# Last block in an order of its own with stores on two queues; a third of block 2's convolution taps by accumulating DMA

## The chip, the core and the metric

The kernel runs on one core of a Trainium2 chip. The core has a matrix engine (TensorE, PE in the profile), VectorE (DVE), ScalarE (ACT), GpSimd (POOL) and SyncE (SP), each with a queue of its own that it works off in order, and 16 DMA engines that all queues share. Waits between engines are semaphores. The metric is device time in microseconds. The median of three runs of the kernel before is 2315.04 us (2314.68 to 2315.27).

## The reference

A causal convolution over seven taps, with one softmaxed filter for each of eight groups of 24 channels, followed by a feed-forward layer with SiLU:

```python
# x: (8, 4096, 192), weight: (8, 7); moe_w_in: (192, 2048), moe_w_out: (2048, 192)
w = np.exp(weight - weight.max(-1, keepdims=True)); w = w / (w.sum(-1, keepdims=True) + 1e-9)
x_pad = np.concatenate([np.zeros((8, 6, 192)), x], axis=1)
idx = np.arange(4096)[:, None] + np.arange(7)[None, :]
out = np.einsum('hk,bskhg->bshg', w, x_pad[:, idx, :].reshape(8, 4096, 7, 8, 24))
h = out.reshape(32768, 192) @ moe_w_in
y = (h / (1 + np.exp(-h))) @ moe_w_out
```

## The kernel before

**Tiling.** The 32768 tokens are worked in 32 blocks of 1024, numbered `b` = 0 to 31, each as two halves of 512 tokens. The 192 channels are three thirds of 64 rows, `k` = 0, 1, 2. A block is loaded (`ld.k`, L156) into a buffer `nat`, of which there are two, so blocks `b` and `b + 2` share one. VectorE turns it (`i.k`, L490) into `xt`, of which there is one; `ha.0` copies the six halo columns (L512). Seven taps (`v.ki`, L526 to L534) make the convolution of third `k`, back in `nat`; `sp.k` (L556) spreads it into `dup`, and `w.i` (L573, L576) makes sums of it in `win`.

**The two matrix products** are done by fast-multiplication schemes that trade products for sums. The weights are combined once, at the start: `combine` by GpSimd (L138) for the groups of the first product, `combine_out` (25 sums) for the second. Block 0 is done plainly, since its weights are not combined yet: `up_plain` (L609) and `down_plain` (L884, the steps `dp`), its output copied by ScalarE (`cp.k`, L899), turned by VectorE (`op.k`, L907) and stored by SyncE (`stp.k`, L916). From block 1 on, `P`, `L` and halves of them are products (L668, L685), `u` ScalarE copies out of PSUM into a pool of ten `u` buffers (L717), `X`, `a`, `b` sums on VectorE (L711), `S` SiLUs (L729); then `t`, `tC`, `tD` (and `tA` on GpSimd) are sums of the SiLU's output (L793), `Q` the 80 products of the second matrix (L804), `O`, `C`, `d` ScalarE copies (L839, L841), `m.i` VectorE sums (L852), `o.i` transposes (L860) and `st.i` four stores each (L867). Each `Q` writes one of the two halves of PSUM's partitions, and two that write different halves can run side by side.

**Taps.** Each tap is a product of a shifted `xt` by a factor for each row. In blocks 1 and 2 ScalarE makes the first tap in a PSUM bank (L526) and VectorE adds the other six (L534). From block 3 on ScalarE makes every product (L529) into a `u` buffer and GpSimd issues a DMA that adds it onto `nat` (L530); the first of the seven goes to `nat` directly. The buffer comes free when the DMA lands, and a DMA onto the same `nat` waits for the one before.

**The order** is written out by hand as strings of steps. Everything that is issued is kept in program order on its engine. `START` does the rest of block 0 along with blocks 1 and 2; in it a bare step belongs to block 2, `-` to block 1, `=` to block 0, `+` to block 3. Then `PLAN` is gone through once for each block, with the prefixes `-`, `=`, `~`, `+`, `*` for one, two, three blocks back and one, two ahead, and for three blocks past the end, so that block 31's last steps run with nothing beside them, in the order that `PLAN` has for every block. The last two groups of weight sums (`both_sides(GROUPS - 1)`, `both_sides(NJ - 1)`: 22 and 19 sums) are issued ahead of `START`.

**In `START`** block 2's taps on VectorE are the last thing before block 0's transposes `op`. SyncE stores block 0 (twelve DMAs) before it issues the other two thirds of block 3's load, and block 3's transposes stand on VectorE ahead of the sums that PE waits for.

Of the kernel before, what the change touches and what calls it, by code (L numbers as in the profile page):

```python
# [17 lines left out]
def kernel(  # L18
# [24 lines left out]
    nc = tc.nc  # L43
# [8 lines left out]
    NK = D // R  # L52
# [4 lines left out]
    NB = NT // TT  # L57
    NCH = DFF // P
    NM = NCH // 2
    NJ = NM // 2  # L60
# [48 lines left out]
        "=dp.10 =dp.11 -v.26 -v.01 -v.02 -v.03 =dp.12 -v.04 =dp.13 -v.05 -v.06 =dp.14 =dp.15 "  # L109
        "=dp.16 -sp.2 =dp.17 =dp.18 =dp.19 =dp.20 -sp.0 i.2 i.1 =dp.21 =dp.22 =dp.23 =dp.24 "  # L110
        "i.0 =dp.25 =dp.26 =dp.27 =dp.28 =dp.29 =dp.30 ha.0 =dp.31 =dp.32 =dp.33 =dp.34 +ld.1 "
        "-w.0 -w.1 =dp.35 =dp.36 v.00 =dp.37 =dp.38 -w.2 -w.3 -w.4 -w.5 =dp.39 =dp.40 =dp.41 "
        "v.01 =dp.42 v.20 =dp.43 =dp.44 v.02 v.03 v.10 v.11 v.12 v.13 v.14 v.15 v.16 v.04 v.05 "
        "v.06 v.22 v.23 v.24 v.25 v.26 =dp.45 =cp.0 =dp.46 =dp.47 =cp.1 v.21 =cp.2 =op.0 =op.1 "
        "=op.2 =stp.0 =stp.1 =stp.2"
    )
    QUEUE = (0, 4, 1, 2, 3)
    CHAIN_BANKS = (
# [11 lines left out]
    def pin(ins):  # L130
        return tc.keep_in_program_order(ins)
# [13 lines left out]
    nats, xts, gs = {}, {}, {}  # L145
# [35 lines left out]
    warm = const.tile([P, 1], F32, name="warm")  # L181
# [9 lines left out]
    pool = Pinned(nc.gpsimd)  # L191
# [142 lines left out]
    def comb(out, u, v, op):  # L334
        pool.tensor_tensor(out, u, v, op=op)
# [3 lines left out]
    def raw(g, i, k, e):  # L339
        a, j, own = chunks(g)[i]  # L340
        return rows(wr[j] if own == e else ws[j], e)[:, a, k, :]

    def combine(g, e):

        def op(sign, to, u, v):
            comb(raw(g, *to, e), raw(g, *u, e), raw(g, *v, e), ALU.add if sign > 0 else ALU.subtract)

        if (g, e) == (SWAP[0], 0):
            op(-1, (2, 1), (1, 0), (1, 2))
            op(-1, (2, 1), (2, 1), (0, 0))  # L350
            op(-1, (2, 1), (2, 1), (0, 1))
        for order in COMBINE[e]:
            op(*order)

    COMBINE = (
        (
# [158 lines left out]
    CONV_BANKS = (2, 3, 4)  # L515
    taken = {}

    def conv(b, k, i):

        src = xts[b][:, k, i : i + TB]  # L520
        dst = nats[b][:, k, :, :].rearrange("p k c -> p (k c)")
        tap = taps[:, k, i : i + 1]
        taken[b, k] = taken.get((b, k), 0) + 1
        acc = banks[CONV_BANKS[k]] if b in (1, 2) else dst
        if i == 0:
            pin(nc.scalar.activation(acc, src, AF.Copy, scale=tap))  # L526
        elif b > 2:
            z = free.pop(0)
            pin(nc.scalar.activation(z, src, AF.Copy, scale=tap))  # L529
            pin(nc.gpsimd.dma_start(out=dst, in_=z, accum_op=ALU.add))  # L530
            free.append(z)
        else:
            pin(
                nc.vector.scalar_tensor_tensor(  # L534
                    out=dst if taken[b, k] == K else acc,
                    in0=src,
                    scalar=tap,
                    in1=acc,
                    op0=ALU.mult,
                    op1=ALU.add,  # L540
                )
            )
# [49 lines left out]
    def rows(t, e):  # L592
        return t[R * e : R * e + R]
# [29 lines left out]
    cmbs, banks = {}, []  # L623

    GROUPS = 5
    SWAP = (4, 14)

    def chunks(g):
        if g == GROUPS - 1:
            return [(1, i, 1) for i in range(3)]  # L630
        return [(0, g, 0), (1, g, 0), (0, g, 1)]
# [99 lines left out]
    def silu_plain(b, i):  # L731
        cols = slice((i - 1) * TB // 2, i * TB // 2) if i else slice(0, TB)
        h = h_of(b, None, int(i > 0))[:, cols]
        pin(nc.scalar.activation(h, plain_bank(b, i)[:, cols], AF.Silu))
# [121 lines left out]
    def turned(i):  # L856
        return mid(2 + i).rearrange("p (k c) -> p k c", c=SQ)

    def turn_out(b, i):
        pin(nc.vector.transpose(mid(2 + i), mid(i - 1)))  # L860

    def store_out(b, i):
        for q in range(P // SQ):
            third, n = OUT_OF[i][q // 2]
            c = R * third + SQ * (q % 2)
            pin(
                nc.sync.dma_start(  # L867
                    out=out_v[2 * b + n][:, :, c : c + SQ],
                    in_=turned(i)[SQ * q : SQ * q + SQ, :, :],
                )  # L870
            )
# [50 lines left out]
    did = set()  # L922
    BACK = {"-": 1, "=": 2, "+": -1, "~": 3, "*": -2}

    def step(b, token):

        if token[0] in BACK:
            b, token = b - BACK[token[0]], token[1:]
        name, _, arg = token.partition(".")
        if b < 0 or b >= NB or (b, token) in did:  # L930
            return
        did.add((b, token))
        digits = [int(c) for c in arg] if arg.isdigit() else []
        if name[0] == "P":
            product(b, digits[0], int(name[1:]))
        elif name == "L":
            plain(b, *digits)
        elif name == "SL":
            silu_plain(b, *digits)
        elif name[0] in "uXabS":  # L940
            sums_h(b, name, *digits)
        elif name[0] == "Q":
            out_product(b, int(name[1:]), *digits)
        elif name[:2] == "tA":
            sum_g(b, int(name[2:]), slice(0, NJ - 1), nc.gpsimd)
        elif name[:2] == "tB":
            sum_g(b, int(name[2:]), slice(NJ - 1, NJ), nc.vector)
        elif name[:2] in ("tC", "tD"):
            i = NJ // 2 if name[1] == "D" else 0
            sum_g(b, int(name[2:]), slice(i, i + NJ // 2), nc.vector)  # L950
        elif name[0] == "t":
            sum_g(b, int(name[1:]), slice(0, NJ), nc.vector)
        elif name in ("O", "C", "d"):
            out_copy(b, token)
        elif name == "m":
            out_sum(b, *digits)
        elif name == "o":
            turn_out(b, *digits)
        elif name == "st":
            store_out(b, *digits)  # L960
        elif name == "dp":
            next(downs)
        elif name == "cp":
            copy_plain(b, *digits)
        elif name == "op":
            turn_plain(b, *digits)
        elif name == "stp":
            store_plain(b, *digits)
        elif name == "go":
            pool.tensor_copy(warm, nats[1][:, digits[0], 0, 0:1])  # L970
            for g in (2, 3):
                for e in range(2):
                    combine(g, e)
        elif name == "ld":
            load(b, digits)
        else:
            {"i": turn_in, "ha": halo_in, "v": conv, "sp": spread, "w": win}[name](
                b, *digits
            )
# [54 lines left out]

    def both_sides(g):
        for e in range(2):
            combine(g, e)

    def some(ups, n):
        for _ in range(n):  # L1040
# [11 lines left out]
    for j, at in ((1, (2,)), (2, (1, 3)), (3, (2,))):  # L1052
# [9 lines left out]
            swapped(3)  # L1062
        if j < NJ - 1:
            both_sides(j)
    both_sides(GROUPS - 1)
    both_sides(NJ - 1)
    for t in [*(f"i.{k}" for k in range(NK)), "ha.0"]:
        step(1, t)
    rounding(7)
# [4 lines left out]
    did.update((0, t.lstrip("-=+~*")) for t in plan)  # L1074
    for t in START.split():
        step(2, t)
    for b in range(1, NB + 4):
        for t in plan:
            step(b, t)


# [28 lines left out]
```

## Time and profile before

| | us |
|---|---|
| median of 3 runs | 2315.04 (2314.68 to 2315.27) |
| the profiled execution | 2315.82 |
| its span, first to last instruction | 2314.1 |
| PE busy | 2288.6 |
| VectorE busy | 2009.3 |
| ScalarE busy | 1550.2 |
| GpSimd busy | 652.4 |

All times below are counted from the start of the span. Matmuls overlap, two in different halves at once, so a busy PE is one on which at least one product runs. `PEld` is PE's loading of weights. `SPq` is SyncE's DMA queue. In a row of the timeline stand start, length, engine, line, operation, what it writes and reads, how many; in brackets how long the engine had been idle and what released it. In a group row stand the count, then the busy time and the mean of one in ns, then the idle time before.

### The profile page before, as it was taken

The page shows a single profiled execution, that of the slowest core. Times are in us where ns is not written, and L with a number is a line of the kernel's source. Part 1 is how long each engine was busy: PE and PEld are TensorE (multiplying, and loading weights), DVE is VectorE, ACT ScalarE, POOL GpSimd, SP SyncE. Part 2 cuts the span into 40 slices and gives each one's busy share as a digit, 9 for nine tenths or more (in the row PEclk, how much of TensorE's full clock was granted, in tenths as well). Part 3 has the DMA queues.
Part 4 walks back from the last instruction along what each step waited for, and adds up shares of the span by engine and source line. Part 5 has one row for each costly group of instructions (what it writes and reads, how often), then busy time and mean ns, then how long its engine had stood idle before and what let it go on. Part 6 is the DMA issues. An engine that isn't in the chain of part 4 may idle for free.

```text
span 2314.1 us, 31693 instructions
## 1 busy us (share of the span) xinstructions
PE 2288.6 (99%) x10622; PEld 922.3 (40%) x10622; DVE 2009.3 (87%) x2271; ACT 1550.2 (67%) x2836; POOL 652.4 (28%) x728
## 2 busy tenths in 40 slices
PE   9999999999999999999999999999999999999997
PEld 4344433444333444334444334443334443344432
DVE  8878888988889888889888889888898888898887
ACT  6267666776666776667776667766677766677642
POOL 5922223222223222233222232222232222332100
PEclk9999999999999999999999999999999999999999
DMA  7355577665667655677655776656676556765411
GB/s 167 69 94 91 97 122 128 113 106 97 107 117 130 107 103 96 115 124 121 107 96 98 123 128 109 104 100 109 117 129 104 102 96 117 126 119 94 75 17 19
DMA packets 526275, 242.65 MB, mean 105 GB/s; under 512 B 431840, under 2 KB 436960, under 8 KB 526112
## 3 DMA queue, kind: packets, MB, share of 16 engines
q0 software_dynamic: 75616, 138.45, 35.3%
q1 hardware_dynamic: 449440, 102.04, 24.8%
q8 instruction: 84, 1.38, 0.2%
q14 instruction: 79, 0.65, 0.1%
q10 hardware_dynamic: 1056, 0.13, 0.0%
HBM read 31.46 MB, written 25.17 MB: 24 GB/s over the span
## 4 chain that ended last, share of the span: by engine, by line
PE 95%; DVE 3%; SPq 1%; ACT 0%; issue 0%; DMA 0%; DVEq 0%
PE ps L804 46%; PE ps L668 44%; PE ps L685 3%; DVE ps L534 1%; DVE two L138 1%; PE ps L994 1%; PE ps L609 0%; SPq L916 0%; DVE mh L138 0%; SPq L156 0%; PE ps L448 0%; DVE t L793 0%; DMA nat<-in_x_dram 0%; ACT g L138 0%; DVE nat L534 0%
## 5 line engine op out<-in xcount | busy, mean ns | idle before, releaser
L530 POOL DMA_DIRECT2D nat<-u x522 | 447.6, 933 | 1244.2 <-ACT u L529 858.6
L804 PE MATMUL ps<-g,wall 128*64 128x512 f32 x1984 | 743.1, 595 | 0.0
L668 PE MATMUL ps<-win,wr 64*128 64x512 f32 x1550 | 685.8, 598 | 2.4 <-ACT u L717 2.4
L668 PE MATMUL ps<-win,ws 64*128 64x512 f32 x1550 | 644.2, 593 | 0.4 <-ACT u L717 0.4
L717 ACT COPY u<-ps 128x512 f32<-128x512 f32 x775 | 439.6, 590 | 109.4 <-issue 58.9
L804 PE MATMUL ps<-g,wx 128*64 128x512 f32 x1240 | 414.5, 592 | 0.0
L668 PE MATMUL ps<-dup,wr 64*128 64x512 f32 x868 | 402.6, 591 | 0.0
L804 PE MATMUL ps<-t,wall 128*64 128x512 f32 x992 | 368.0, 594 | 0.5 <-DVE t L793 0.5
L529 ACT ACTIVATE u<-xt,taps 128x512 f32<-128x512 f32 x522 | 353.9, 716 | 0.7
L668 PEld LDWEIGHTS ps<-win,wr 64*128 64x128 f32 x1550 | 256.0, 186 | 221.0 <-issue 131.5
L711 DVE TENSOR_TENSOR g<-u,ps 128x512 f32<-128x512 f32 x465 | 309.7, 683 | 31.5 <-PE ps L668 29.2
L729 ACT ACTIVATE g<-ps 128x512 f32<-128x512 f32 x465 | 279.9, 602 | 39.6 <-PE ps L668 39.0
L668 PEld LDWEIGHTS ps<-win,ws 64*128 64x128 f32 x1550 | 257.1, 187 | 121.5 <-issue 94.5
L729 ACT ACTIVATE g<-g 128x512 f32<-128x512 f32 x465 | 280.9, 631 | 34.5 <-DVE g L711 34.5
L804 PEld LDWEIGHTS ps<-g,wall 128*64 128x64 f32 x1984 | 215.7, 137 | 220.9 <-issue 211.7
L711 DVE TENSOR_TENSOR ps<-u,ps 128x512 f32<-128x512 f32 x310 | 214.9, 694 | 92.4 <-PE ps L668 33.1
L668 PE MATMUL ps<-dup,ws 64*128 64x512 f32 x682 | 271.2, 591 | 7.4 <-DVE ps L711 7.4
L804 PE MATMUL ps<-t,wx 128*64 128x512 f32 x744 | 267.0, 594 | 1.3 <-ACT ps L841 1.3
L793 DVE TENSOR_TENSOR t<-g 128x512 f32<-128x512 f32 (+1 forms) x186 | 240.9, 1309 | 5.0 <-DVE g L793 0.5
L839 ACT COPY cmb<-ps 64x512 f32<-64x512 f32 x124 | 72.1, 581 | 238.7 <-PE ps L804 215.6
L793 DVE TENSOR_TENSOR t<-g,t 128x2048 f32<-128x2048 f32 x93 | 212.9, 2290 | 9.0 <-PE ps L804 7.8
L804 PEld LDWEIGHTS ps<-g,wx 128*64 128x64 f32 x1240 | 129.5, 137 | 210.1 <-issue 210.1
(103 smaller groups left out, 2477.3 us busy)
## 6 DMA issues: line engine op xcount, KB each, us to landing
nat<-u POOLq DMA_DIRECT2D x522, 256.0 KB, 4.2
dup<-nat SPq DMA_DIRECT2D x345, 128.0 KB, 2.6
nat<-in_x_dram SPq DMA_DIRECT2D x382, 64.0 KB, 3.9
out_dram<-yx SPq DMA_DIRECT2D x248, 64.0 KB, 2.1
out_dram<-cmb SPq DMA_DIRECT2D x124, 64.0 KB, 4.5
raw<-in_moe_w_out_dram SPq DMA_DIRECT2D x8, 384.0 KB, 4.6
g<-in_moe_w_in_dram SPq DMA_DIRECT2D x8, 192.0 KB, 5.3
ws<-wr POOLq DMA_DIRECT2D x8, 192.0 KB, 4.9
```

Source lines behind the costliest of these rows:

```text
L138: return lambda *args, **kw: pin(getattr(self.engine, name)(*args, **kw))
L529: pin(nc.scalar.activation(z, src, AF.Copy, scale=tap))
L530: pin(nc.gpsimd.dma_start(out=dst, in_=z, accum_op=ALU.add))
L534: nc.vector.scalar_tensor_tensor(out=dst if taken[b, k] == K else acc, in0=src, scalar=tap, in1=acc, op0=ALU.mult, op1=ALU.add,)
L668: nc.tensor.matmul(to[:, cols], raw(g, *LEFT[e][r], e), rhs[:, cols], start=first, stop=True, skip_group_check=True,)
L685: nc.tensor.matmul(plain_bank(b, n and 1 + e)[:, cols], rows(wr[j] if own == e else ws[j], e)[:, a, k, :], rows(dups[b], e)[:, SLOT[e][2 * ...
L711: pin(nc.vector.tensor_tensor(out_, u, v, op=op))
L717: pin(nc.scalar.copy(us[b, g, o][:, cols], t1[:, cols]))
L729: pin(nc.scalar.activation(h, src, AF.Silu))
L793: pin(engine.tensor_tensor(g_part(to, js), g_part(u, js), g_part(v, js), op=op))
L804: nc.tensor.matmul(out_bank(node), out_form(OUT_FORMS[r])[:, j, :], g_part(OPERAND[r], j), start=first, stop=True, skip_group_check=True,)
L839: pin(nc.scalar.copy(to(), out_bank(node)))
```

## The change

Three things.

1. Third `k` = 2 of block 2 is convolved as in the blocks from 3 on: ScalarE makes the first tap in `nat` and six products in `u` buffers, and GpSimd issues six accumulating DMAs. VectorE's six taps for it go. Thirds 0 and 1 of block 2 stay on VectorE.
2. The 41 weight sums that were issued ahead of `START` become a generator `late`, and steps `go.n` in `START` take them from it, the first digit of `n` being the count: 13 ahead of `v.21`, then 5, 5, 5, 5, 4 and 4, with one of the taps `v.22` to `v.26` between each two. On GpSimd the sums keep their order, and the six DMAs stand among them: behind the 13th, 18th, 23rd, 28th, 33rd and 37th. The taps `v.20` to `v.26` now come before `w.0`, and so before `v.00` and `v.10` on ScalarE.
3. The steps of block 31 that `FINISH` names (its 80 `Q`, nearly all its `t`, the copies, `m`, `o`, `st`, and the last few SiLUs and sums ahead of them) are held back while `PLAN` runs, and done after it in `FINISH`'s order. Of the four stores of each `st.i` in block 31, the second and fourth are issued by ScalarE's queue. The steps of block 30 that stood among them come earlier, its last transpose `o.3` and stores `st.3` among them.

In the built programs the order of PE, VectorE and ScalarE between block 3 and block 31's `Q` products is the same as before.

```diff
-        "-w.0 -w.1 =dp.35 =dp.36 v.00 =dp.37 =dp.38 -w.2 -w.3 -w.4 -w.5 =dp.39 =dp.40 =dp.41 "
-        "v.01 =dp.42 v.20 =dp.43 =dp.44 v.02 v.03 v.10 v.11 v.12 v.13 v.14 v.15 v.16 v.04 v.05 "
-        "v.06 v.22 v.23 v.24 v.25 v.26 =dp.45 =cp.0 =dp.46 =dp.47 =cp.1 v.21 =cp.2 =op.0 =op.1 "
-        "=op.2 =stp.0 =stp.1 =stp.2"
+        "go.9 go.4 v.20 v.21 go.51 v.22 go.52 v.23 go.53 v.24 go.54 v.25 go.41 v.26 go.42 -w.0 "
+        "-w.1 =dp.35 =dp.36 v.00 v.10 =dp.37 =dp.38 -w.2 -w.3 -w.4 -w.5 =dp.39 =dp.40 =dp.41 "
+        "v.01 =dp.42 =dp.43 =dp.44 v.02 v.03 v.11 v.12 v.13 v.14 v.15 v.16 v.04 v.05 v.06 "
+        "=dp.45 =cp.0 =dp.46 =dp.47 =cp.1 =cp.2 =op.0 =op.1 =op.2 =stp.0 =stp.1 =stp.2"
+    )
+    FINISH = (
+        "Q17.1 Q4.0 S1.2 Q17.0 Q4.3 S0.0 Q17.3 Q3.0 Q17.2 a0.2 S5.2 S4.2 Q4.1 Q4.2 O.0 tC3 "
+        "Q6.0 Q12.0 Q3.1 Q12.1 Q11.2 Q3.2 Q11.3 tC4 S0.2 tD2 C.0 tD4 tD3 Q5.1 Q12.3 Q5.0 t5 "
...
+        "m.0 d.A Q8.1 d.B Q2.0 d.b Q7.1 m.4 m.1 Q8.0 o.2 Q1.2 Q7.2 m.2 Q2.1 Q19.2 Q2.3 m.5 "
+        "st.2 Q8.3 Q8.2 o.1 st.1 m.3 o.3 st.3"
     )
...
         def op(sign, to, u, v):
             comb(raw(g, *to, e), raw(g, *u, e), raw(g, *v, e), ALU.add if sign > 0 else ALU.subtract)
+            return g
...
         for order in COMBINE[e]:
-            op(*order)
+            yield op(*order)
...
-        acc = banks[CONV_BANKS[k]] if b in (1, 2) else dst
+        by_dma = b > 2 or (b, k) == (2, NK - 1)
+        acc = dst if by_dma or not b else banks[CONV_BANKS[k]]
         if i == 0:
             pin(nc.scalar.activation(acc, src, AF.Copy, scale=tap))
-        elif b > 2:
+        elif by_dma:
             z = free.pop(0)
             pin(nc.scalar.activation(z, src, AF.Copy, scale=tap))
             pin(nc.gpsimd.dma_start(out=dst, in_=z, accum_op=ALU.add))
...
             c = R * third + SQ * (q % 2)
+            queue = nc.scalar if b == NB - 1 and q % 2 else nc.sync
             pin(
-                nc.sync.dma_start(
+                queue.dma_start(
...
         elif name == "go":
-            pool.tensor_copy(warm, nats[1][:, digits[0], 0, 0:1])
-            for g in (2, 3):
-                for e in range(2):
-                    combine(g, e)
+            some(late, digits[0])
...
+    late = (op for g in (GROUPS - 1, NJ - 1) for e in range(2) for op in combine(g, e))
...
-    both_sides(GROUPS - 1)
-    both_sides(NJ - 1)
...
+    last, held = NB - 1, FINISH.split()
+    did.update((last, t) for t in held)
     for b in range(1, NB + 4):
         for t in plan:
             step(b, t)
+    did.difference_update((last, t) for t in held)
+    for t in held:
+        step(last, t)
```

## The prediction

> **What bounds the kernel now.** First the page (shares, chain of waits), then busy time by stretches, to see where the bounding engine is not busy.
>
> ```profile
> span 2314.1 us, 31693 instructions
> PE 2288.6 (99%) x10622; PEld 922.3 (40%) x10622; DVE 2009.3 (87%) x2271; ACT 1550.2 (67%) x2836; POOL 652.4 (28%) x728
> PE 95%; DVE 3%; SPq 1%; ACT 0%; issue 0%; DMA 0%; DVEq 0%
> ```
>
> ```profile
> 100.00:150.00 50.00, 39.75 (x164) 23.11 (x162) 27.28 (x41) 29.77 (x57) 22.49 (x28) 0.90 0.33 55
> 150.00:200.00 50.00, 50.00 (x230) 18.37 (x228) 44.54 (x44) 31.21 (x57) 12.96 (x16) 1.00 0.66 117
> 2264.13:2301.74 37.61, 35.86 (x161) 11.46 (x160) 28.76 (x19) 9.15 (x17) 0.00 (x0) 1.00 0.05 8
> 2301.74:2314.10 12.36, 0.00 (x1) 0.00 (x0) 4.46 (x7) 0.00 (x0) 0.00 (x0) 0.70 0.42 64
> ```
>
> After the length come busy us of PE, PEld, DVE, ACT, POOL, then PE's clock and the DMA share; the last two stretches are from block 31's first L804 product to its last, and what follows. PE is idle for 2314.1 - 2288.6 = 25.5 us in all, of which 10.25 lie between 100 and 150 us, 1.75 in the last products and 12.36 after them, so between block 1 and the last block there is next to none: whatever moves PE's restart before 150, or shortens the end, goes whole into the time. The change touches both. The chain of waits around the first:
>
> ```profile
> 103.75 0.72 DVE osb L907
> ...
> 116.15 2.30 DMA nat<-in_x_dram
> 119.21 0.67 DVE xt L490
> 119.88 0.60 DVE ps L711
> 120.52 4.63 PE ps L668 x9
> ```
>
> VectorE ends block 2's taps (L534), turns block 0's output (L907), SyncE stores it (L916) and only then loads block 3; VectorE, in order, turns block 3 (L490) before the sum (L711) for which PE waits until 120.52.
>
> **Part 1: block 2's third k = 2.** Six taps leave VectorE, one tap and six products enter ScalarE, six accumulating DMAs enter GpSimd's queue.
>
> ```profile
> 90.04 6.15 DVE L534 SCALAR_TENSOR_TENSOR ps<-xt,taps,ps 128x512 f32<-128x512 f32 x8
> ...
> 103.75 1.89 DVE L907 STREAM_TRANSPOSE osb<-cmb 128x512 f32<-128x512 f32 x3
> ...
> 86.64 1.91 ACT L526 ACTIVATE ps<-xt,taps 128x512 f32<-128x512 f32 x3 [4.40 <-DVE win L573]
> ...
> 101.60 0.58 ACT L899 COPY cmb<-ps 128x512 f32<-128x512 f32 x1 [0.27 <-PE ps L884]
> ...
> 104.48 7.88 SPq L916 DMA_DIRECT2D out_dram<-osb  x12
> ...
> 84.62 0.63 SPq L512 DMA_DIRECT2D xt<-xt  x1
> ```
>
> VectorE: 18 taps run from 90.04 to 103.75, 0.762 us each; six fewer are -4.57 us. ScalarE gives part of it back. Its block 2 taps start at 86.64, when the halo copy issued at 84.62 has landed, and the built order puts k = 2's first tap and all six products before `v.00`. Three took 1.91 us, 0.6 apart; I take 0.62 (bounds 0.60 and the 0.72 of one alone), so `v.00` ends at 86.64 + 7 x 0.62 + 0.7 = 91.7 and VectorE starts its taps there, not at 90.04: +1.7 (1.5 to 2.3). They end at 91.7 + 12 x 0.762 = 100.8; the transposes start at 100.9 instead of 103.75 (-2.85). The last copy of block 0's output ends at 102.18, past the start of the third transpose, but eight stores stand before the third's, so SyncE does not wait. SyncE's queue has the same order, so its stores, loads and PE's restart move by the same 2.85, unless the stores meet the new DMAs.
>
> ```profile
> q0 software_dynamic: 75616, 138.45, 35.3%
> ...
> L530 POOL DMA_DIRECT2D nat<-u x522 | 447.6, 933 | 1244.2 <-ACT u L529 858.6
> ...
> nat<-u POOLq DMA_DIRECT2D x522, 256.0 KB, 4.2
> ...
> 82.41 2.36 POOL L138 TENSOR_TENSOR wr<-wr,wr 64x128 f32<-64x128 f32 x5
> ...
> 98.59 0.73 POOL L138 TENSOR_TENSOR wall<-wall 128x256 f32<-128x256 f32 x1
> ...
> 116.55 0.72 POOL L138 TENSOR_TENSOR wx<-zeros,wx 128x256 f32<-128x256 f32 x1
> ...
> 130.91 0.92 POOL L530 DMA_DIRECT2D nat<-u  x1 [13.64 <-ACT u L529]
> ...
> DMA to landing us min/median/max: 3.2/4.1/6.5
> ```
>
> (The last row is of the u buffers from 60 to 230 us.) The first of the five at 82.41 is the 13th of GpSimd's last 41 weight sums, done at 82.9. Then its first new DMA waits for a product that ends at 86.64 + 0.62 + 0.72 = 88.0: 5 us of stall, with 28 weight sums and the 25 output sums behind it. The six add to one buffer, so each also waits for the one before to land: 4.2 us apart (3.2 to 6.5), while the four or five sums between (about 0.5 each) and an issue of 0.93 take 3.4. The sixth is issued at 88.0 + 5 x 4.2 = 109.0, the weight sums end at 109.0 + 0.93 + 4 x 0.46 = 111.8 instead of 98.5, and the output sums, 18.7 us, at 130.5 instead of 117.3. Who waits for that?
>
> ```profile
> 132.70 0.59 PE L668 MATMUL ps<-dup,wr 64*128 64x512 f32 x1
> ...
> 137.15 1.07 ACT L717 COPY u<-ps 128x512 f32<-128x512 f32 x2
> ```
>
> The first product that reads the last group is the one at 132.70: 18 us of room. The group before it is complete two sums after the second DMA, near 97, and is read only behind PE's last L884 product, which the copy at 101.60 waits for. The output forms are read by L804 products, later still. Block 3's first DMA, at 130.91 so far, is then wanted near 128.6 and goes at 130.5; its buffer is wanted by the ScalarE copy of 137.15 (134.8 after the shift), and it lands at 130.5 + 4.2 = 134.7. No cost, but no room either; at 3.2 us a landing there are 6 us.
>
> ```profile
> 104.48:116.64 12.16, 6.81 (x20) 2.50 (x20) 1.75 (x3) 3.40 (x8) 11.61 (x18) 0.95 0.64 96
> ```
>
> An accumulating DMA costs all 16 engines 0.353 x 2314 / 522 = 1.56 us. Two of the six (near 104.8 and 109) fall among the stores and loads, which fill 0.64 of the engines over their 12.16 us: 0 to 3.1 us of delay, and I take 0.8, since most fits into the idle share. Restart: -2.85 + 0.8 = -2.05, bounds -3.1 and +0.3.
>
> ```profile
> 113.00:113.80 0.80, 0.09 (x1) 0.00 (x0) 0.00 (x0) 0.00 (x0) 0.75 (x2) 1.00 0.61 94
> ...
> 115.40:116.20 0.80, 0.00 (x0) 0.00 (x0) 0.00 (x0) 0.00 (x0) 0.80 (x2) 0.50 0.86 134
> ...
> 125.00:125.80 0.80, 0.80 (x5) 0.36 (x3) 0.10 (x1) 0.00 (x0) 0.00 (x0) 0.61 0.00 0
> ```
>
> The granted clock halves at 115.4, after 2.3 us without a product, and comes back at 125.6, 5.1 us after the restart; those 5.1 us do 2.5 us of work. With the gap cut to 5.3 us it may stay as it is, or the slow stretch shortens: I take -0.25 (0 to -2.5). Part 1: -2.3.
>
> The Trainium skill (TensorE: Matmul & The Clock Gate, "Part 1: The HAM clock gate") says the clock is judged over free-running windows of about 3.4 us and is released after one busy window. The trace agrees: 115.4 to 125.6 is three such windows. By that rule, with the same phase, a restart at 118.4 comes just before the boundary at 118.8, and the clock returns at 122.2: 3.8 slow us instead of 5.1, -0.65 where I took -0.25.
>
> **Part 2: the last block.** Block 31's 80 final products, its sums, copies and stores go in an order of their own; half the stores go to ScalarE's queue.
>
> ```profile
> 2280.92 20.84 PE ps L804 x96
> ...
> 2276.25 2.29 DVE L793 TENSOR_TENSOR t<-g,t 128x2048 f32<-128x2048 f32 x1 [1.00 <-PE ps L804]
> ...
> 2301.79 1.39 DVE L852 TENSOR_TENSOR cmb<-cmb,ps 64x512 f32<-64x512 f32 x2 [1.26 <-PE ps L804]
> ...
> 2305.64 0.66 DVE L860 STREAM_TRANSPOSE yx<-cmb 128x512 f32<-128x512 f32 x1
> ...
> 2305.14 1.94 SPq L867 DMA_DIRECT2D out_dram<-yx  x4
> 2307.18 2.10 SPq L867 DMA_DIRECT2D out_dram<-cmb  x4
> 2309.38 2.10 SPq L867 DMA_DIRECT2D out_dram<-yx  x4
> ```
>
> PE: products go in pairs, one to each half of the columns; 96 rows (two a product) are 24 pairs in 20.84 us, 0.868 a pair. In the built order of before all 80 pair up, 40 x 0.868 = 34.7, yet 37.6 pass: 2.9 us are waits. In the new order a product of one half often follows one of the same half; taken strictly in order that makes 37 pairs and 6 alone, 43 x 0.868 = 37.3. Its waits: the sum at 2276.25 loses its 1.00 us wait in the new order and has one more transpose ahead (0.66), so it starts at 2275.9; the pair nearest to waiting, the 28th, is due at 2264.13 + 27 x 0.868 = 2287.6 and reads the fourth sum after it, ready at 2275.9 + 5 x 2.32 = 2287.5. ScalarE's copies end 0.6 us after their banks, a pair or more before they are read. I add 0.2. PE ends at 2301.6, as before (2301.74); bounds 2300.3, were lone halves filled, and 2303.4, with 1.8 us of such waits as now.
>
> After it, before: five adds and three transposes on VectorE until 2306.3, twelve stores in one queue, the last issued at 2311.0, 3.1 us before the end. After: only one add (0.68) and one transpose (0.66) depend on the last product, the rest having operands up to 3 us earlier: 2303.0. Of the last four stores each queue has two, 0.53 apart: the last goes at 2303.5, the end is 3.1 later, 2306.6, and 0.3 for both queues at once: 2306.9. That is -7.2 (-5.4 to -8.5). Block 30's last transpose, moved ahead of the sums, and its stores lie in VectorE and SyncE time that PE does not wait for; uncovered it is 0.7.
>
> The DMA share while twelve stores ran in series:
>
> ```profile
> 2307.00:2308.00 1.00, 0.00 (x0) 0.00 (x0) 0.00 (x0) 0.00 (x0) 0.00 (x0) 0.50 0.82 122
> ```
>
> The Trainium skill (DMA: Bandwidth & Descriptors, "Issuing engines are not separate DMA queues") says that a second issuing engine saves only the sequencer's time, since all queues share 16 DMA engines. At a share of 0.82 four stores need 4 x 0.53 x 0.82 = 1.7 us of those engines however they are issued, 0.35 more than my 1.06 + 0.3, so the end by that rule is 2307.3. The order, and not the second queue, carries this part.
>
> **Sum.** -2.3 - 7.2 = -9.5 on the profiled execution: 2315.82 to 2306.3, its span 2314.1 to 2304.6. That execution stands 0.78 over the median shown, 2315.04; on the median, 2305.5.
>
> **Rivals.** (a) The start gives nothing: new DMAs slow SyncE's stores by the full 3.1 us, or ScalarE is later than counted. For it: that share of 0.64. Against: only two of six fall there. Only part 2 is left: 2315.0 - 7.2 = 2307.8. (b) The end is bound by PE and VectorE: lone halves plus waits as today, +1.8 us: 2307.3, and with (a) 2309.6. (c) PE's clock stays full over the shorter gap: -2.25 more, 2303.2. Against it: it halved after 2.3 us of idling. (d) Slower: GpSimd's queue turns critical. If its chain lands at 6.5 us, the most seen, the sixth DMA goes at 120.5, output sums end at 142.0, block 3's first DMA lands at 148.5 and ScalarE's copy, with every copy and so PE behind it, is 13.7 late: 2305.5 + 13.7 = 2319.2. It decides from 4.2 us a landing on, and turns the sign from 5.8. Against it: from 88 to 100 us the DMA engines are almost empty, so landings should be near 3.2 to 4.2.
>
> **How the numbers follow.** Forecast 0.66, (a) 0.13, (b) 0.10, (c) 0.06, (d) 0.05. Range: best bounds -8.2 and -3.8 give 2303.0; (a) with (b) gives 2309.6, taken to 2310. A difference under 0.2%, 4.6 us, counts as no change here. Forecast, (a), (b) and (c) are all past it, but (a) and (b) together with a little of (d) are not: faster 0.90, same 0.06, slower 0.04.
>
> **What would show it.** VectorE's taps of block 2 end near 100.8 and the first L907 store goes near 101.6; PE restarts near 118.4 (right), or at 120 or later ((a), (d)). GpSimd's output sums end near 130 and no ScalarE copy waits for a DMA at 135. At the end PE stops near 2299.3 in the new span, with about 5.3 us behind it instead of 12.36. Wrong would be a PE idle after 150 us, or more than 7 us behind the last product.

## The result, and the profile after

The changed kernel takes 2308.80 us in the median (2307.61 to 2312.21, 17 runs) where the kernel before takes 2315.27 (2314.32 to 2316.99, 17 runs) beside it: a ratio of 0.9973, 95% interval 0.9965 to 0.9980. That is 6.5 us faster, with 9.5 forecast. The profiled execution has a span of 2306.9 us and a time of 2308.6.

The page of the changed kernel: its span, the busy time of the engines, and the shares of the chain of waits.

```profile
span 2306.9 us, 31722 instructions
PE 2289.8 (99%) x10622; PEld 934.1 (40%) x10622; DVE 2005.2 (87%) x2265; ACT 1554.2 (67%) x2842; POOL 654.8 (28%) x734
PE 94%; DVE 3%; SPq 1%; ACT 1%; issue 0%; DMA 0%; ACTq 0%; DVEq 0%
```

The instruction counts are those of the change: six fewer on VectorE, six more on ScalarE and on GpSimd. PE is idle for 2306.9 - 2289.8 = 17.1 us instead of 25.5. Its busy time by stretches, columns as in the prediction:

```profile
100.00:150.00 50.00, 40.92 (x171) 24.14 (x169) 26.22 (x40) 30.32 (x59) 31.83 (x45) 0.90 0.48 79
2300.70:2306.90 6.20, 0.00 (x0) 0.00 (x0) 1.40 (x2) 0.00 (x0) 0.00 (x0) 0.82 0.61 90
```

The first stretch still has 9.1 idle us (10.25 before), the one behind the last product 6.2 (12.36 before). So nearly all of the idle time saved is at the end. The start, in the order of time (start, length, engine and line; in brackets the idle time before, and what ended it):

```profile
88.19 0.92 POOL L542 DMA_DIRECT2D nat<-u  x1 [5.53 <-ACT u L541]
...
91.56 6.17 DVE L546 SCALAR_TENSOR_TENSOR ps<-xt,taps,ps 128x512 f32<-128x512 f32 x8 [2.23 <-ACT ps L538]
...
100.67 1.89 DVE L920 STREAM_TRANSPOSE osb<-cmb 128x512 f32<-128x512 f32 x3
...
101.40 7.56 SPq L929 DMA_DIRECT2D out_dram<-osb  x12
...
108.07 0.87 POOL L542 DMA_DIRECT2D nat<-u  x1 [1.71 <-DMA nat<-u]
...
109.00 5.92 SPq L166 DMA_DIRECT2D nat<-in_x_dram  x8
...
116.92 1.30 DVE L501 STREAM_TRANSPOSE xt<-nat 128x512 f32<-128x512 f32 x2 [13.77 <-DMA nat<-in_x_dram]
...
118.87 1.22 PE L680 MATMUL ps<-dup,ws 64*128 64x512 f32 x1 [6.26 <-DVE ps L723]
```

The same two rows of the kernel before, the loads and the transposes of block 3:

```profile
112.40 4.24 SPq L156 DMA_DIRECT2D nat<-in_x_dram  x8
...
118.57 1.31 DVE L490 STREAM_TRANSPOSE xt<-nat 128x512 f32<-128x512 f32 x2 [12.34 <-DMA nat<-in_x_dram]
```

VectorE turns block 0's output 3.08 us earlier than before (100.67 against 103.75) and the stores go 3.08 earlier (101.40 against 104.48); but block 3 is turned only 1.65 earlier (116.92 against 118.57): from the first store to these transposes it takes 15.5 us instead of 14.1. PE restarts 1.65 earlier (118.87 against 120.52).

### The profile page after: what moved, and what is told of

Read it like the earlier page. It is cut to its first block, busy times and chain, and to the rows that moved or that the text cites. A ratio compares the mean times of both kernels' runs of the same rounds, so it can differ in the third digit from the quotient of the medians.

```text
span 2306.9 us, 31722 instructions
## 1 busy us (share of the span) xinstructions
PE 2289.8 (99%) x10622; PEld 934.1 (40%) x10622; DVE 2005.2 (87%) x2265; ACT 1554.2 (67%) x2842; POOL 654.8 (28%) x734
## 4 chain that ended last, share of the span: by engine, by line
PE 94%; DVE 3%; SPq 1%; ACT 1%; issue 0%; DMA 0%; ACTq 0%; DVEq 0%
PE ps L816 46%; PE ps L680 45%; PE ps L697 3%; DVE ps L546 1%; DVE two L148 1%; DVE t L805 1%; PE ps L1004 1%; PE ps L621 0%; SPq L166 0%; DVE mh L148 0%; SPq L929 0%; DVE g L805 0%; DMA nat<-in_x_dram 0%; DVE xt L501 0%; ACT g L148 0%
## 5 line engine op out<-in xcount | busy, mean ns | idle before, releaser
L542 POOL DMA_DIRECT2D nat<-u x528 | 452.6, 928 | 1243.3 <-ACT u L541 822.8
L816 PE MATMUL ps<-g,wall 128*64 128x512 f32 x1984 | 743.7, 595 | 0.0
L816 PE MATMUL ps<-g,wx 128*64 128x512 f32 x1240 | 415.2, 592 | 0.0
L680 PE MATMUL ps<-dup,wr 64*128 64x512 f32 x868 | 402.8, 591 | 0.0
L816 PE MATMUL ps<-t,wall 128*64 128x512 f32 x992 | 369.1, 594 | 0.4 <-DVE t L805 0.4
L816 PEld LDWEIGHTS ps<-g,wall 128*64 128x64 f32 x1984 | 215.6, 137 | 222.2 <-issue 213.0
L816 PE MATMUL ps<-t,wx 128*64 128x512 f32 x744 | 267.3, 594 | 0.0
L816 PEld LDWEIGHTS ps<-g,wx 128*64 128x64 f32 x1240 | 129.4, 137 | 211.2 <-issue 210.3
```

The lines of the kernel that those rows point to most:

```text
L680: nc.tensor.matmul(to[:, cols], raw(g, *LEFT[e][r], e), rhs[:, cols], start=first, stop=True, skip_group_check=True,)
L816: nc.tensor.matmul(out_bank(node), out_form(OUT_FORMS[r])[:, j, :], g_part(OPERAND[r], j), start=first, stop=True, skip_group_check=True,)
```

## The experiments

**e1: the end alone.**

```diff
 # before.py; START and conv stay
+    FINISH = ( ... )
+            queue = nc.scalar if b == NB - 1 and q % 2 else nc.sync
+    last, held = NB - 1, FINISH.split()
...
```

> The kernel of before with only the new order of block 31's final products and the two store queues. Theory (the two parts are independent; the start is worth about 1.9 us in the span, the end 6.1): PE reaches the last block's first final product where it did before, near 2264, stops near 2301.8, the span ends 6.2 us behind that: about -6, 2309.2. Rival 1 (the parts as sized in the prediction, end -7.2): 2308.0. Rival 2 (the end gives less than it seems, since the profiled execution of the changed kernel began 0.3 us early by chance and lost 0.75 us on the way): -5.5 or less, 2309.8.

Measured: 2308.09 us (2307.81 to 2309.93, 6 runs) against 2315.19; ratio 0.9970 (0.9959 to 0.9982), -7.1. The whole gain of the change is there without its first part: the changed kernel's 2308.80 is not below it. The last block runs nearly as in the changed kernel.

**e2: the start alone.**

```diff
 # after.py
-    FINISH = ( ... )
-            queue = nc.scalar if b == NB - 1 and q % 2 else nc.sync
+            queue = nc.sync
 # and the closing loop as before
```

> The changed kernel without the new end: old order and one store queue in block 31. Theory: VectorE's taps of block 2 end near 100.7, PE restarts near 118.9 instead of 120.5, and the slow stretch of the clock moves along with it: -1.9 in the span of which some 0.3 is a chance offset at the start, so -1.6 on the median, 2313.7. Rival 1 (the start as predicted, -2.3): 2313.0. Rival 2 (rival (a) of the prediction, the start gives nothing and the profiled gain is chance): within 0.5 of before.

Measured: 2314.73 us (11 runs), -0.46 against 2315.19, ratio 0.9998 (0.9989 to 1.0006): by the median rival 2, no measurable gain. Yet in its trace PE restarts at 118.68, as early as in the changed kernel. So the theory of the start holds up to 150 us, and in this execution something takes the gain back later. (It took 2316.18 us, 1.45 more than the median of its kernel.) The chain of waits of e2 shows where (start, length, what):

```profile
1749.92 18.40 PE ps L670 x85
1768.32 5.77 DMA dup<-nat
...
1774.12 0.70 DVE win L575
...
1774.84 0.70 DVE win L575
...
1775.68 1.95 PE ps L670 x6
```

In all other blocks the 96 products of that piece follow without a break. Here PE waits for VectorE, and VectorE for a copy of block data that took 5.77 us to land. Counting from the start of one block's 96 products to the next, e2 loses 1.42 us in this block and 0.34 in the one from 342.68; all others take 70.35 us.

**e3: the last block's stores on one queue.**

```diff
 # after.py
-            queue = nc.scalar if b == NB - 1 and q % 2 else nc.sync
+            queue = nc.sync
```

> The changed kernel with all stores of block 31 on SyncE's queue. With two queues the last store is issued at 2302.63, and the 16 DMA engines are full (share 0.93 to 1.01) from 2302 to 2305. Theory (the engines' time bounds the end): one queue issues the last store near 2304.0, each lands as fast as before (2.0 us), the end is 3.1 us behind: 2307.1 in the span, +0.2 (-0.2 to +0.5). Rival (the issuing queue bounds the end): the last store goes 1.4 us later and lands as late after its issue as now: +1.4.

Measured: 2308.74 us (7 runs), ratio 0.9973 (0.9962 to 0.9983), as the changed kernel. The end of the changed kernel, and then that of e3:

```profile
2300.74 0.69 DVE L864 TENSOR_TENSOR cmb<-cmb,ps 64x512 f32<-64x512 f32 x1 [0.26 <-PE ps L816]
2301.46 0.71 DVE L872 STREAM_TRANSPOSE yx<-cmb 128x512 f32<-128x512 f32 x1
2302.20 0.87 SPq L880 DMA_DIRECT2D out_dram<-yx  x2
2302.20 0.96 ACTq L880 DMA_DIRECT2D out_dram<-yx  x2
...
DMA to landing us min/median/max: 2.1/2.7/3.1
```

```profile
2301.69 0.69 DVE L864 TENSOR_TENSOR cmb<-cmb,ps 64x512 f32<-64x512 f32 x1 [0.26 <-PE ps L816]
2302.41 0.71 DVE L872 STREAM_TRANSPOSE yx<-cmb 128x512 f32<-128x512 f32 x1
2303.50 2.10 SPq L880 DMA_DIRECT2D out_dram<-yx  x4
...
DMA to landing us min/median/max: 1.8/2.0/2.0
```

From the last sum to the end of the span it is 2306.9 - 2300.74 = 6.16 us with two queues and 2308.2 - 2301.69 = 6.51 with one. The second queue issues faster, but each store lands later: 0.35 us of this one execution is what remains of its worth, and by the medians nothing does (2308.74 against 2308.80). The expectation that the time of the 16 DMA engines bounds the end is borne out, and the rival's +1.4 is not.

**e4: block 3's loads ahead of block 0's stores.**

```diff
 # after.py, START
-        "... =dp.34 +ld.1 "
+        "... =dp.34 +ld.1 +ld.0 +ld.2 "
```

> The changed kernel with block 3's other eight loads issued with the first four, near 88 us, ahead of block 0's stores; nothing else. Theory (what holds PE until 118.87 is SyncE's order of work: stores, then loads, then VectorE's transposes): VectorE turns block 3 right behind block 0's output, near 104, the wait of 6.26 us before 118.87 goes and the clock stays full or nearly so, up to 8.7 us; but block 3's first accumulating DMA stands behind GpSimd's output sums until 129.6, lands near 133, and ScalarE's copy behind it would then be wanted at 127 to 129, so 4 to 6 us come back as a new wait: -3 to -5, 2304 to 2306. Rival 1 (GpSimd is not in the way): -8, 2301. Rival 2 (the loads are hidden anyway, PE waits for something else at 118.87): no change.

Measured: 2310.16 us (11 runs), ratio 0.9980 (0.9971 to 0.9989): slower than the changed kernel by 1.4. PE's wait until 118.87 is gone, and this one has come:

```profile
131.21 0.82 POOL L542 DMA_DIRECT2D nat<-u  x1
...
134.52 1.07 ACT L729 COPY u<-ps 128x512 f32<-128x512 f32 x2 [8.14 <-DMA nat<-u]
```

GpSimd's output sums hold block 3's first accumulating DMA, as expected, at a higher price (8.1 us, where 4 to 6 were expected), and PE's clock then halves from 132.1 to 139.0.

**e6: e1 with the same two loads moved.** VectorE keeps all taps and GpSimd has no new DMAs.

```diff
 # e1, START
-        "... =dp.34 +ld.1 "
+        "... =dp.34 +ld.1 +ld.0 +ld.2 "
```

> The start of before (all taps of block 2 on VectorE, no new DMAs) with block 3's loads ahead of block 0's stores, and the new end. Theory (PE's gap before 120 is SyncE's order; GpSimd's output sums end at 117.3 there, so its DMA for block 3 is not late): VectorE turns block 3 right behind block 0's output, near 107, PE restarts near 114 instead of 119 to 120, the clock may stay full: -5 to -8 against e1 at 2308.1, so 2300 to 2303. Rival (something else holds PE, as in e4): 2308 or more.

Measured: 2298.71 us (2298.49 to 2298.98, 5 runs) against 2315.19; ratio 0.9929 (0.9917 to 0.9942). It beats both kernels, the changed one by 10.1 us. Its stretch from 100 to 150, and the transposes:

```profile
100.00:150.00 50.00, 47.18 (x212) 26.68 (x210) 38.04 (x55) 39.09 (x75) 25.19 (x31) 1.00 0.48 86
```

```profile
104.59 7.27 SPq L927 DMA_DIRECT2D out_dram<-osb  x12
...
105.68 1.85 DVE L500 STREAM_TRANSPOSE xt<-nat 128x512 f32<-128x512 f32 x3
```

Block 3 is turned some 11 us earlier than in the changed kernel, PE idles for 2.8 us instead of 9.1, and the clock stays at 1.00.

**e7: e4 with 16 of the 25 output sums behind block 3's first accumulating DMA.**

```diff
 # e4
-                                combine_out()
+                                some(outs, 9)
 # PLAN
-        "-S3.0 -w.5 +v.11 -P3.1 ..."
+        "-S3.0 -w.5 +v.11 -os -P3.1 ..."     # -os: the other 16
```

> e4 with all but nine of GpSimd's 25 output sums behind block 3's first accumulating DMA; nothing else. In e4 that DMA stood behind them until 131.21, and ScalarE's copy and PE waited 8.1 us for it. Theory (the order in GpSimd's queue is what e4 lost): the DMA goes near 120, the copy finds its buffer at 126, the wait and the slow clock from 132 go: -8 to -11 against e4 at 2310.2, so 2299 to 2302. Rival (the output sums, ending near 133, are late for the last products of block 1, or the next DMAs queue behind them): only -3 to -5, 2305 to 2307.

Measured: 2300.59 us (2299.95 to 2302.18, 5 runs), ratio 0.9938 (0.9925 to 0.9950). That DMA goes at 121.94 instead of 131.21, and 9.6 us come back: what e4 lost was the order in GpSimd's queue. Also here e6, without the change's first part, is 1.9 us faster.

**e11: the loads alone, on the kernel before.**

```diff
 # before.py, START
-        "... =dp.34 +ld.1 "
+        "... =dp.34 +ld.1 +ld.0 +ld.2 "
```

> The kernel of before with block 3's loads ahead of block 0's stores, and nothing else (old start, old end). Theory (e6 less the end's 7.1): e6 is 2298.7, so 2305.8, with PE restarting near 111 and the clock full throughout. Rival (the gain needs the new end as well): 2307 or more.

Measured: 2305.04 us (2304.78 to 2305.24, 5 runs) against 2315.32; ratio 0.9955 (0.9942 to 0.9969). Its first run of 96 products behind PE's restart starts 11.0 us earlier than that of before (132.97):

```profile
121.93 20.89 PE ps L668 x96
```

All its later blocks take the usual 70.35 us, so here what moves PE's restart does go into the time nearly whole. Together with e6 it gives a further price of the end: 2298.71 - 2305.04 = -6.3.

**e8: the last two of the six DMAs.**

```diff
 # after.py, START
-        "... v.24 go.54 v.25 go.41 v.26 go.42 ..."
+        "... v.24 go.54 go.41 go.42 ..."
```

> The changed kernel with two of the six products and accumulating DMAs of block 2's third k = 2 left out (the taps 5 and 6 are missing from that third). In the changed kernel block 0's first store goes at 101.40 and block 3 is turned at 116.92, 15.5 us later; in before and e1 these were 14.1 and 13.2. Theory (the last DMAs contend with stores and loads): with none issued after 99.7 the distance is 13.2 to 14.1 again and PE restarts near 117.3. Rival (the stores and loads are slow for another reason): 15.4 as in e2 and e3.

The kernel does something else than this text says: a block's plan does what its start has left undone, so the two taps were not left out but came later, behind GpSimd's output sums. One run, 2318.35 us.

```profile
126.14 0.82 POOL L542 DMA_DIRECT2D nat<-u  x1
129.43 0.59 ACT L729 COPY u<-ps 128x512 f32<-128x512 f32 x1 [8.08 <-DMA nat<-u]
129.89 0.85 POOL L542 DMA_DIRECT2D nat<-u  x1 [2.92 <-DMA nat<-u]
```

It shows what rival (d) of the prediction feared, by another way: two of the DMAs stand late in GpSimd's queue, and ScalarE's copy and PE wait 8 us. On the question that it was made for it says little: from the first store (100.87) to the transposes (115.60) it is 14.7 us, but e5, e10 and e12 below have 14.7, 15.0 and 14.7 with all six. And its fourth DMA, issued at 100.18, landed at 103.84, among the stores, so that it is no kernel without a meeting.

**e5, e9, e10, e12: where the start's gain goes.** In the changed kernel's own trace the block from 342.24 takes 71.01 us, not 70.35 (its busy time by engine, columns as in the prediction):

```profile
342.24:413.25 71.01, 71.01 (x331) 30.66 (x330) 62.17 (x70) 49.62 (x91) 19.18 (x20) 1.00 0.64 110
```

PE counts as busy in all of it. The block is longer although PE is never idle: behind a late sum its products no longer start two by two, and a busy PE is one on which at least one runs. VectorE pauses in this block, once with no releaser that the profile shows and once after its own sum; and GpSimd issues the first accumulating DMA of the block from 1749.79 late, after an idle time of 4.52 us where the other blocks have 3.2:

```profile
365.35 0.69 DVE L585 TENSOR_TENSOR win<-dup 128x512 f32<-128x512 f32 x1 [0.46 <-issue]
...
403.88 0.69 DVE L723 TENSOR_TENSOR ps<-u,ps 128x512 f32<-128x512 f32 x1 [0.46 <-DVE cmb L864]
...
1764.63 1.75 POOL L542 DMA_DIRECT2D nat<-u  x2 [4.52 <-ACT u L729]
```

The kernel before has one such pause on VectorE, at another place, and PE does not feel it:

```profile
2005.16 2.29 DVE L793 TENSOR_TENSOR t<-g 128x2048 f32<-128x2048 f32 x1 [0.46 <-PE ps L804]
```

The change alters the number of instructions of VectorE, ScalarE and GpSimd by six each. So three kernels (e5, e10, e12, "shifted" below) change these counts with tiny operations in waits that exist anyway, and e9 leaves them alone.

```diff
 # after.py, START; pd: fills on VectorE, pg: on GpSimd, pa: copies on ScalarE
-        "go.9 go.4 v.20 v.21 ..."
+        "pd.6 go.9 go.4 pg.4 v.20 v.21 ..."          # e5
+        # e10: as e5, with one 64x1 transfer on GpSimd's queue behind the fills
+        "pd.6 go.9 go.4 pa.8 pg.4 v.20 v.21 ..."     # e12
```

> The changed kernel with six tiny fills on VectorE (near 86 us, where it waits for ScalarE anyway) and four on GpSimd (near 84 us, in its wait for the first product), so that VectorE's count of instructions is again that of before and GpSimd's stream is shifted. The profiled execution of the changed kernel loses 0.67 us of PE in the block from 342 us and 0.1 in the one from 1750: VectorE pauses 0.46 us at 365.35 and at 403.88, and GpSimd issues the first accumulating DMA of one block 1.3 us late (1764.63); e2 and e3 show the same places, up to 1.9 us in all, while before and e1 show none that PE feels. Theory (an engine pauses at places counted in its own stream, and the change moved these places onto the path): with the counts shifted all blocks of PE are 70.35 us apart again, -0.7 to -1.9, 2307 to 2308. Rival (the pauses belong to the changed work or to the moment, not to the count): the same places lose the same, 2308.8.

> The changed kernel once more, unaltered, beside the next two. Theory (its lost 0.3 to 2 us of PE between 340 and 1825 come back in every execution): 2308.8, and two blocks of PE (the fourth and the twenty-fourth after 130) longer than 70.35 us. Rival (a chance of that one execution): other blocks, or none.

> e5 with one tiny transfer more on GpSimd's queue in the same wait near 84 us. In e5 VectorE's pause at 403.88 had gone from PE's path (it shows at 212.8 and 2180.6, harmless), but GpSimd's first accumulating DMA of the block from 1749 was again late (1763.62 after an idle 4.61 instead of 3.23), and that block lost 0.47. Theory (that place is counted in GpSimd's DMAs, which the change raised by six, and which the four fills left alone): one DMA more moves the late one to the DMA before it, which has 14 us of idle queue ahead; the block is 70.35 us again, and the median falls by about 0.5 against e5 at 2307.5: 2307.0. Rival (it is counted in ScalarE's instructions, or belongs to the block): the same DMA is late again and the block loses 0.1 to 1.5.

> e5 with eight tiny copies more on ScalarE, in its idle time of 4.5 us before 86.5. In e5, e9 and e10 GpSimd's first accumulating DMA of the block from about 1749 is late by the same 1.3 us, whatever was added to GpSimd's own stream or to its DMAs. Theory (the place is counted in ScalarE's instructions, of which the change added six): eight more move it away, that DMA follows an idle time of 3.2 us as in the other blocks, the block is 70.35 us, and the median is 2307.0 (e5: 2307.5). Rival (something else than these three counts): the same DMA is late again.

Measured: e9 2308.72 us (7 runs), e5 2307.50 (5), e10 2307.82 (5), e12 2307.59 (6). From the traces, in us. A block's start is that of its run of 96 products; a loss is what a block takes over 70.35 us (the first block's 0.1 less, the same in all of them, is not counted):

| kernel | start of the first such run after PE's restart | lost near 342 | lost from 1670 to 1825 |
|---|---|---|---|
| before / e1 (old start) | 132.97 / 131.46 | 0 / 0 | 0 / 0 |
| changed / e2 | 131.11 / 131.55 | 0.66 / 0.34 | 0.11 / 1.42 |
| e3 / e9 | 130.94 / 130.31 | 0.33 / 0.34 | 1.51 / 1.90 |
| e5 / e10 / e12 (shifted) | 130.73 / 131.18 / 129.32 | 0 / 0 / 0 | 0.47 / 0.16 / 0 |

e9 has its losses in the blocks that e2 and e3 have them in, so they are no chance of one execution. VectorE's pause, set against the same operation in the other blocks (0.35 us later), stands at the same two places in every kernel with the same start: 403.4 and 1198.2 in e3, 402.8 and 1197.6 in e9. The fills move both, to 212.8 and 2180.6 in e5, 213.3 and 2180.8 in e10, 211.4 and 2178.7 in e12, all of them off PE's path, and the loss near 342 is gone: that these two places are fixed by the program, and that the change put one on the path, is borne out. What counts is not VectorE's operations alone: e4 and e7, with those of the changed kernel and its loads elsewhere, pause at 486.8 and 1741.2, 479.7 and 1734.1. The pause at 365.35 is in the changed kernel's trace only, and not in that of e9, the same program; about half of the 0.66 us is its share.

What these pauses have in common stands in the DMA queues. From 404.5 to 406 us the changed kernel's profile has one transfer of 8 KB on the queue that it calls `instruction`:

```profile
q14 instruction: 1, 0.01, 1.3%
```

It starts 0.9 us after the operation at 403.88. In each of the ten traces with the new start such a transfer follows both of VectorE's pauses, 0.5 to 1.0 us after the late operation's start, and in before and e1 1.6 to 1.9 us after it. The queue starts one in about 29 us, so this is hardly chance. That loading instructions is what holds VectorE up is not shown; the pause at 365.35 has none within 8 us.

The late DMA is another matter. In e12:

```profile
1762.21 1.75 POOL L542 DMA_DIRECT2D nat<-u  x2 [4.61 <-ACT u L729]
```

It is late by the same 1.3 us whether GpSimd's instructions (e5), its DMAs (e10) or ScalarE's instructions (e12) are shifted: those three theories fell, and what it goes by stays open. No transfer on that queue q14 starts within 8 us of it. What it costs PE differs from execution to execution, 0 to 1.9 us; in e2 it came by a copy that landed late. The 0 of e12 is from its fastest run (2305.81, median 2307.59). The three shifted kernels are faster than e9 by 0.9 to 1.2 us (their 16 runs together have a median of 2307.5, the 24 of the changed program with e9 2308.7); part of that is an earlier restart (117.7 to 118.1 instead of 118.6 to 118.9), which isn't explained.

## Why the prediction was right, and where not

**The forecast.** 2308.8 lies in the range and 3.3 above the forecast: the start gave about nothing where -2.3 was forecast, the end some 0.7 less than -7.2, and the kernel before stood 0.2 higher than in the runs shown. The range held since it had room for a start that gives nothing, not because the text foresaw why.

**VectorE and ScalarE of part 1: right.** Taps from 91.56 (forecast 91.7), transposes at 100.67 (100.9), first store at 101.40 (101.6).

**GpSimd: right.** First DMA at 88.19 (88.0), sixth at 108.07 (109.0), block 3's DMA at 129.59 (130.5), and ScalarE's copy at 135.29 without a wait. "No cost, but no room either" was right too: e4 moved PE ahead by some 9 us and fell into just that wait, and so did e8, which put two DMAs behind the sums.

**The stores and loads: mis-sized.** I took 0.8 us for their meeting with the DMAs (0 to 3.1). From the first store to block 3's transposes it is 14.1 (before) and 13.2 (e1), against 15.5, 15.4, 15.4 and 15.2 (changed, e2, e3, e9): 1.7 more in the mean of these four, and 1.0 to 1.4 more in e5, e10 and e12. SyncE takes about 0.5 us to issue one of these DMAs. Its longest, first of before, then two of the changed kernel (start, length):

```profile
108.72 2.00 SPq L916
```

```profile
106.11 1.10 SPq L929
...
109.00 2.19 SPq L166
```

Every kernel has one of over 1 us between 108 and 110. The new start adds an earlier one, each time with an accumulating DMA between issue and landing: at 106.11 in the changed kernel, with the DMA of 103.67 that landed 3.86 us later, and at 101.77 in e8, with that of 100.18. This earlier one makes some 0.7 to 0.9 us of the difference and fits the meeting with the DMAs, though no run has the new start without them; the rest stays open. That only the last two DMAs matter, as I counted, was not shown: in e8 it was the fourth.

**The clock: -0.25 was no more than a guess at a phase.** The granted clock (the third column from the end) where it falls, at PE's restart and where it comes back; first the changed kernel, then e9, the same program:

```profile
113.25:113.50 0.25, 0.00 (x0) 0.00 (x0) 0.00 (x0) 0.00 (x0) 0.17 (x2) 0.63 1.07 168
118.75:119.00 0.25, 0.13 (x2) 0.13 (x2) 0.25 (x2) 0.00 (x0) 0.25 (x1) 0.50 0.00 0
123.50:123.75 0.25, 0.25 (x4) 0.12 (x1) 0.00 (x0) 0.00 (x0) 0.25 (x1) 0.89 0.00 0
```

```profile
115.00:115.25 0.25, 0.00 (x0) 0.00 (x0) 0.00 (x0) 0.00 (x0) 0.17 (x2) 0.75 0.71 110
118.75:119.00 0.25, 0.14 (x2) 0.14 (x2) 0.25 (x2) 0.00 (x0) 0.17 (x2) 0.50 0.00 0
121.75:122.00 0.25, 0.25 (x4) 0.17 (x1) 0.00 (x0) 0.25 (x2) 0.24 (x1) 0.60 0.00 0
```

PE restarts at 118.87 and 118.86, yet the clock is back at 123.5 in the one and at 121.9 in the other: the slow stretch lasts 10.2 or 6.8 us and begins at 113.3 or 115.1. From its restart on PE works 4.7 us at half speed in the one and 3.1 in the other, so 0.8 us between two executions hang on this alone. The rule of the Trainium skill (TensorE: Matmul & The Clock Gate, "Part 1: The HAM clock gate") that the windows run freely and one busy window releases the clock agrees with both: three windows and two. The prediction worked out -0.65 by it for one phase; the phase could not be known. Before 150 us the change gained 132.97 - 131.11 = 1.86 us between the two profiled executions. Over the kernels above the old start (before, e1) has its first run of 96 products at 132.2 in the mean and the new one (changed, e2, e3, e9) at 131.0: 1.2. This is a small difference beside the 1.5 by which before and e1, with the same start, differ.

**The step that failed:** "whatever moves PE's restart before 150, or shortens the end, goes whole into the time". For this start that did not hold: later blocks took longer, by 0.8, 1.8, 1.8 and 2.2 us in the four traces with the new start, 1.6 in the mean, against a gain of 1.2. (These four executions are 0.75 us slower in the mean than the medians of their kernels, so at the median the loss is less.) So the start moved PE's restart and the time did not follow: -0.46 by the medians with the old end (e2 against before), +0.7 with the new one (changed against e1), neither clear of the spread of the runs. The text had called an idle PE after 150 us a sign that it is wrong. That sign was badly chosen: the changed kernel's PE is idle nowhere between 150 us and block 31's last products, and yet its blocks lose 0.8 us; only their length shows it. Where all blocks keep their 70.35 us the step holds: e11 moved PE by 11.0 us and the time by 10.3. Rival (a) had about the right amount, 2307.8, by a mechanism that is only in part the one found: longer stores and loads took some of what VectorE gave, but PE's restart did come earlier, and that gain went in later blocks.

**Part 2: right in kind, too large by 0.7 in the medians and 1.1 in the trace.** Three pairs of medians give -7.1 (e1, before), -5.9 (changed, e2) and -6.3 (e6, e11), some -6.5 in the mean. From block 31's first L804 or L816 product to the end of the span it is 2314.1 - 2264.13 = 50.0 us before and 2306.9 - 2263.02 = 43.9 after: -6.1. PE needs 2300.70 - 2263.02 = 37.7 us for the last products (forecast 37.3 and 0.2), with one wait for a sum:

```profile
2284.43 2.29 DVE L805 TENSOR_TENSOR t<-g 128x2048 f32<-128x2048 f32 x1 [0.46 <-DVE g L805]
```

That is the fourth sum after the one named, ready at 2286.7 in a span whose last block starts 1.1 us earlier, some 0.3 us later than reckoned; the pair nearest to waiting was well chosen. The larger miss is behind PE: 6.2 us, not 5.3. The transposed tile is ready at 2302.2, 1.5 us behind PE where 1.4 was forecast. The last store is issued at 2302.63, also as forecast, but the end comes 4.3 us after it and not 3.1 + 0.3: the stores land up to 3.1 us after their issue (2.0 in e3, with one queue), as eight stores of two queues meet:

```profile
2302.00:2303.00 1.00, 0.00 (x0) 0.00 (x0) 0.17 (x1) 0.00 (x0) 0.00 (x0) 1.00 0.95 140
2303.00:2304.00 1.00, 0.00 (x0) 0.00 (x0) 0.00 (x0) 0.00 (x0) 0.00 (x0) 1.00 0.93 135
2304.00:2305.00 1.00, 0.00 (x0) 0.00 (x0) 0.00 (x0) 0.00 (x0) 0.00 (x0) 0.83 1.01 144
```

The DMA share (next to last column) is full until 2305. The Trainium skill (DMA: Bandwidth & Descriptors, "Issuing engines are not separate DMA queues") lets a second issuing engine save only the time it takes to initiate a DMA, and the trace agrees: by that rule the end was to come 0.4 us later than in my sum, 0.9 was measured, and e3 puts the queue's whole worth at 0.35 or less. "The order, and not the second queue, carries this part" is shown by e3.

**Two slips without consequence.** The range's lower end uses -8.2 and -3.8, while the bounds worked out are -8.5 for the end and -3.1 with up to -2.5 for the start. And the group of weight sums before the last is complete four sums after the second DMA, not two; that was at 94.9, well before its first reader.

## What to carry to other kernels

When an engine waits behind a queue, ask first whether the queue's order is needed: two thirds of a block's load moved ahead of stores gave 10.3 us (e11), where taking work off the engine in front of them gave nothing that could be measured. Work handed to an engine with idle time also lengthens that engine's in-order queue and meets others' transfers, so look for what stands behind it there (e4, e8). And a gain at the start of a long steady loop counts only if every later round still takes its old time: compare the rounds' starts in both traces before believing it, since the bounding engine can count as busy all the while.

## What the runs showed of the hardware that was not expected

VectorE runs an operation 0.35 us late at one or two places of a run without a wait that explains it. Both traces of the changed program, and those of e2, e3 and e8 with the same start, have the same two places; six tiny instructions more move them, and one in PE's path costs 0.33 us. A transfer on the `instruction` queue follows each of them, by 0.5 to 1.0 us with the new start; that it is the cause is not shown. GpSimd's first accumulating DMA of one block is issued 1.3 us late in all ten traces with the new start, and in none of the four with the old one (before, e1, e6, e11); no shift that was tried moved it. Two executions of one program had PE's slow stretch 10.2 and 6.8 us long, although PE restarted at the same time in both (118.87 and 118.86).
